# A causal retention layer with a gated convolution block: a hand-written tail, and transposes of four steps by DMA

## Chip, cores and metric

The kernel runs on one core of a Trainium2 chip. The metric is the device time of one execution in microseconds; lower is better. The kernel before is given by the median of 8 runs, and by one profiled execution, from which all durations and views come.

## What is computed

The first stage is a retention: attention without softmax, with a decay that depends on the head, over 8 batches, 8 heads, 576 positions and a head width of 64. The second is a gated linear unit whose gate is the sigmoid of a causal convolution with 5 taps for each channel.

```python
scores = scale * q @ k.T                       # [8, 8, 576, 576]
ret = scores * gamma[h] ** (i - j)             # for i >= j, else 0
x = (ret @ v).transpose(0, 2, 1, 3).reshape(8, 576, 512)
gate_pre = sum(conv_w[k] * xp[:, k:k + 576] for k in range(5))   # xp: 4 rows of zeros ahead of x
out = (sigmoid(gate_pre) * (x @ w_val)) @ w_out
```

## The kernel before

**Steps.** The retention is chunked: a step handles all 8 heads of 256 positions of one batch, or, for the last 64 positions, of two batches at once. There are 20 steps, 16 full ones and 4 short ones (6, 9, 16 and 19). The order of the last ones is: 15 (batch 6, second half), 16 (short, batches 4 and 5), 17 and 18 (batch 7), 19 (short, batches 6 and 7). Each step has a list of letters (`FULL`, `PART`) that fixes the order of its parts on all engines:
- `load` (L94), called four steps ahead: SyncE issues the DMA loads of keys, queries and values into `kf`, `qf`, `vf`, each in a rotation of four buffers.
- `cast` (L222), two steps ahead: GpSimd scales keys and queries by the decay and turns all three into bf16 (`kb`, `qb`, `vb`).
- `T`, `transp` (L245), one step ahead: TensorE transposes keys and queries into PSUM, 8 matrices of 128x128 for each of the two in a full step and 4 in a short one. ScalarE copies the keys to `kt`, VectorE the queries to `qt`.
- `Sa`, `Sb`, `Sr` (L269): the scores on TensorE from `kt` and `qt`; VectorE multiplies them by the causal mask into `am` (L289).
- `X`, `XS`: the state of the next step, its sums `sn` on VectorE and bf16 copies `w` on ScalarE.
- `I`, `Va`, `Vb`, `Vr`: the part from the state and the part from the scores, added in PSUM in `o`.
- `E` (L362 ff.): VectorE and ScalarE copy `o` to the rows `xt` (or `xr` for a short step, where GpSimd also copies four padding columns, L374).
- `B`: `push_block` makes a block of the second stage. A number in the list is a budget in microseconds for work from the blocks' queue.

**Blocks.** A block is 512 or 256 rows of the second stage. Its parts are: `conv` (L434), which does two of the four channel groups with 40 small matmuls against diagonal matrices and then two sigmoids on ScalarE; `val` (L480), a product with `w_val` on TensorE which VectorE multiplies by the gate into `z`; `outp` (L493), four matmuls with `w_out`, an evacuation `ob` on ScalarE and a store that SyncE issues. There are 12 blocks, numbered from 0. Blocks 8 to 11 (`DV`) have only channel groups 0 and 1 of the convolution on TensorE. For group 2 ScalarE makes five products and GpSimd adds them; for group 3 VectorE does five multiply-adds (`tap`, L450). `gate` (L468) then makes the sigmoids, and `pull` issues taps at given places.

**Order.** Every engine executes its instructions in the order in which the program issues them. Nothing is reordered, so an instruction that waits holds up what stands behind it on its engine; this holds for the DMA issues of SyncE too. After step 19 the rest of the queue is worked off in its order:

```python
tail[0] = 0
while work or late:
    if not work:
        work.extend(late)
        late.clear()
    fill(1.0)
```

At that point the queue holds two `outp` of block 7, `conv`, four `val` and four `outp` of block 8, and the same parts of blocks 9, 10 and 11 (256 rows each). In the tail, the PSUM tiles of `val` and `outp` come in pairs from two pools of two (`scp`, `opp`); the convolution uses a third pool of four (`glp`).

Of the kernel before, what the change touches and what calls it, by code (L numbers as in the profile page):

```python
# [31 lines left out]
def kernel(  # L32
# [14 lines left out]
    P = 128  # L47
# [12 lines left out]
    TPS, DSS, CAP = False, False, 2.0  # L60
    PB, EV, TE = [4, 2, 2], "DA", "AD"
    C1, LO = "PPP", "1vo23"
    SPL, REMD = 0, [2, 0, 2, 0]
    VC = "P"
    PULL = [2, 3]
    LATE = True
    DV, OSB = [8, 9, 10, 11], 4
    cst = ctx.enter_context(tc.tile_pool(name="cst", bufs=1))
    ld = ctx.enter_context(tc.tile_pool(name="ld", bufs=4))
    cs = ctx.enter_context(tc.tile_pool(name="cs", bufs=4))  # L70
# [151 lines left out]
    def cast(s):  # L222
        u, bb, n = steps[s]
        r = st[s]
        R = 1 if bb is None else 2
        shp = [P, R, H, D]
        f0 = n * 2
        nb = 2 if bb is None else 4
        kb = cs.tile(shp, BF16, tag=f"kb{R}", name="kb", bufs=nb)
        qb = cs.tile(shp, BF16, tag=f"qb{R}", name="qb", bufs=nb)  # L230
        vb = cs.tile(shp, BF16, tag=f"vb{R}", name="vb", bufs=nb)

        how = C1 if s == 1 else "PP" + VC[s % len(VC)]
        for e, dst, src, f in ((how[0], kb, r["kf"], fk), (how[1], qb, r["qf"], fq)):
            (nc.vector if e == "D" else nc.gpsimd).tensor_tensor(  # L235
                dst, src.rearrange("p h r d -> p r h d"),
                f[:, f0:f0 + R, :].unsqueeze(3).to_broadcast(shp), op=ALU.mult)
        vsrc = r["vf"].rearrange("p h r d -> p r h d")
        if how[2] == "A":
            nc.scalar.copy(vb, vsrc)  # L240
        else:
            nc.gpsimd.tensor_copy(vb, vsrc)  # L242
        r.update(qb=qb, kb=kb, vb=vb)

    def transp(s, which="kq"):  # L245
        if s >= NS:
            return
        r = st[s]
        R = 1 if steps[s][1] is None else 2
        for nm in which:  # L250
            src = r[nm + "b"]
            tp = (scp if TPS else glp).tile([P, HP, R, P], BF16, tag="sc" if TPS else "gps", name="tp" + nm)
            for hp in range(HP):
                for rr in range(R):
                    nc.tensor.transpose(tp[:, hp, rr, :],  # L255
                                        src[:, rr, 2 * hp:2 * hp + 2, :].rearrange("p a d -> p (a d)"), ident)
            t = at.tile([P, HP, R, P], BF16, tag=f"{nm}t{R}", name=nm + "t", bufs=1 + R)
            copy(TE[nm == "q"], t, tp)
            r[nm + "t"] = t
# [140 lines left out]

    blk = [0]
    tail = [None]

    def gps(shape, name):

        pools = [(glp, "gps")] if tail[0] is None else [(scp, "sc"), (opp, "o")]
        if tail[0] is not None:
            tail[0] += 1
        pool, tag = pools[(tail[0] or 0) // 2 % len(pools)]
        return pool.tile(shape, F32, tag=tag, name=name)  # L410

    def push_block(xt, bi, t0, segs):


        me = blk[0]
        blk[0] += 1
        g = {}
        z = {}
        n = segs[0][2]
        J = len(segs)  # L420
        N = n * J

        def win(d, off):
            if bi is None:
                return xt[:, d, :, off:off + n]
            return xt[:, d, bi, t0 + off:t0 + off + n]

        def fold(ap):
            return ap.rearrange("p (j t) -> p j t", j=J) if bi is None else ap

        shape = [P, N]

        def conv(d0):
            cps = [glp.tile(shape, F32, tag="gps", name="cps") for _ in range(2)]  # L434
            for kk in range(KC):
                for p2 in range(2):
                    for i in range(2):
                        for r in range(2):
                            nc.tensor.matmul(fold(cps[i][HS[r ^ i]]),  # L439
                                             lhsT=diag[HS[r], p2, kk, d0 + i, :], rhs=win(d0 + i, kk)[HS[r]],  # L440
                                             start=(kk == 0 and p2 == 0),
                                             stop=(kk == KC - 1 and p2 == 1), skip_group_check=True)
            for i in range(2):
                gt = gl.tile([P, DM], F32, name="gt")[:, 0:N]
                nc.scalar.activation(gt, cps[i], AF.Sigmoid)  # L445
                g[d0 + i] = gt

        acc = {}

        def tap(d, kk):  # L450

            if kk == 0:

                acc[d] = glp.tile([P, DM], F32, tag="gps", name="acc")[:, 0:N] \
                    if d == 3 and tail[0] is not None else gl.tile([P, DM], F32, name=f"accs{d}", bufs=2 if d == 2 else 1)[:, 0:N]
            if d == 2:

                y = acc[d] if kk == 0 else gl.tile([P, DM], F32, name="prod", bufs=3)[:, 0:N]
                nc.scalar.activation(fold(y), win(d, kk), AF.Copy, scale=cw[:, kk, d:d + 1])  # L459
                if kk:  # L460
                    nc.gpsimd.tensor_tensor(acc[d], acc[d], y, op=ALU.add)  # L461
            elif kk == 0:
                nc.vector.tensor_scalar(fold(acc[d]), win(d, 0), cw[:, 0, d:d + 1], None, op0=ALU.mult)
            else:
                nc.vector.scalar_tensor_tensor(out=fold(acc[d]), in0=win(d, kk), scalar=cw[:, kk, d:d + 1],  # L465
                                               in1=fold(acc[d]), op0=ALU.mult, op1=ALU.add)

        def gate(d):  # L468
            while pend[me, d]:
                pend[me, d].pop(0)()  # L470
            gt = gl.tile([P, DM], F32, name="gt")[:, 0:N]
            if d == 2:
                nc.scalar.activation(gt, acc[d], AF.Sigmoid)
            else:
                for y in range(2):
                    nc.scalar.activation(gt[HS[y]], acc[d][HS[1 - y]], AF.Sigmoid)
            g[d] = gt
            gated.add((me, d))

        def val(d):  # L480
            if onv and d in (1, 2):
                gate(d + 1)
            if d == 0:
                z[0] = zp.tile([P, DT, DM], BF16, name="zt")
            vp = gps(shape, "vps")
            for do in range(DT):
                nc.tensor.matmul(fold(vp), lhsT=wval[:, do, d, :], rhs=win(do, PAD),  # L487
                                 start=(do == 0), stop=(do == DT - 1))
            nc.vector.tensor_tensor(z[0][:, d, 0:N], g[d], vp, op=ALU.mult)  # L489
            if tail[0] is not None and d in PULL:  # L490
                pull(2 if d < 3 else 3, KC)

        def outp(m):  # L493
            op = gps([P, DM], "ops")
            for d in range(DT):
                nc.tensor.matmul(op, lhsT=z[0][:, d, m * P:(m + 1) * P], rhs=wout[:, d, :],  # L496
                                 start=(d == 0), stop=(d == DT - 1))
            ob = os_.tile([P, DM], F32, name="ob")
            nc.scalar.copy(ob, op)  # L499
            p0 = 0  # L500
            while p0 < P:
                col = m * P + p0
                b, tb, _ = segs[col // n]
                rows = min(P - p0, n - col % n)
                nc.sync.dma_start(out=out[b, tb + col % n:tb + col % n + rows, :], in_=ob[p0:p0 + rows])
                p0 += rows

        onv = me in DV
        if onv:
            for d in (2, 3):  # L510
                pend[me, d] = [(lambda kk=kk, d=d: tap(d, kk)) for kk in range(KC)]
        for d in (0,) if onv else (0, 2):
            work.append((conv, d, 0.15 + 2.15 * N / 512))
        work.extend(late)
        late.clear()
        for d in range(DT):
            work.append((val, d, 0.05 + 0.84 * N / 512))

        (late if (onv and LATE) or (xts[0] is xt and not bi and not t0) else work).extend(
            (outp, m, 0.9) for m in range(N // P))  # L520
# [16 lines left out]
    def first(op, hv, e):  # L537
# [56 lines left out]
        elif op == "E":  # L594
            xts[0] = xtb[0]
            for x in range(2):
                copy(e[x], xtb[0][:, ps, 0, PAD + x * P:PAD + (x + 1) * P].rearrange("p a (i r) -> p a r i", r=2),
                     r["o", hv][x].rearrange("p a (r i) -> p a r i", r=2))

    LOOK = 4  # L600
    credit = [0.0]
    usable = ["conv0"]
# [27 lines left out]
    for s in range(NS):  # L630
# [3 lines left out]
            load(s + LOOK)  # L634
        if s > 1 and s + 2 < NS:
            cast(s + 2)
        for op in (PART if bb is None else FIRST if s == 0 else SECOND if s == 1 else FULL[n]):
            if op[:2] in ("D0", "D2"):
                prep_diag(int(op[1]), nc.vector if op[3] == "D" else nc.gpsimd)
            elif s == 0 and ":" in op:  # L640

# [53 lines left out]
            else:  # L695
                fill(float(op))
    tail[0] = 0
    while work or late:
        if not work:
            work.extend(late)  # L700
            late.clear()
        fill(1.0)


# [28 lines left out]
```

## Time and profile before

| what | value |
|---|---|
| median of 8 runs | 184.0 us (182.37 to 184.83) |
| the profiled execution | 183.5 us |
| its span, first to last instruction | 181.7 us |
| TensorE busy | 156.1 us (86%) |
| VectorE, ScalarE, GpSimd busy | 122.8, 105.8, 104.5 us |
| last evacuation `ob` ends, in the span | 177.5 us |
| granted clock of TensorE | 0.996 |

The page of a profile lists the busy time of each engine, the span in 40 slices, the DMA queues, the chain of work that ended last, and the costliest groups of instructions. In a timeline a line gives start, length, engine, source line, operation, what is written and read, shapes and the count; SPq is SyncE's queue, which issues DMAs. The landing time of a DMA is the time from the start of its issue to the moment when its data are there. A busy matmul is modelled with its pipeline, so the starts of two groups in a row tell more than their lengths.

### The profile page before, as it was taken

Reading aid. Unit: us, or ns where it says so; the run is one execution under the profiler, and the core shown is the slowest. Engines: PE = TensorE matmul, PEld = TensorE weight load, DVE = VectorE, ACT = ScalarE, POOL = GpSimd, SP = SyncE. Lnnn points to the kernel's source line nnn. Section 1 sums busy time; section 2 is a strip of 40 time slices with the busy share of each in tenths; the row PEclk is TensorE's granted clock in tenths of the full one; section 3 lists DMA queues with packets and bytes.
Section 4 is the critical chain, followed back from the end, with each engine's and each line's share of the span. In section 5 each row is a group of like instructions: output and inputs, shape, how many; then the busy total and the mean of one; then the engine's idle time right before and its main releaser. Section 6 shows DMA issues by size and latency. Waiting matters only on the chain.

```text
span 181.7 us, 7665 instructions
## 1 busy us (share of the span) xinstructions
PE 156.1 (86%) x3320; PEld 104.6 (58%) x3345; DVE 122.8 (68%) x233; ACT 105.8 (58%) x214; POOL 104.5 (58%) x101
## 2 busy tenths in 40 slices
PE   0479779967899998899999999989999979999970
PEld 0347556745576666565666596575677534556630
DVE  2968573668669645967489769549679880658830
ACT  6654766454551756257346765464587324989860
POOL 5059299986568957488937780886307600145420
PEclk9999999999999999999999999999999999999998
DMA  5999999999999998999999889996340005032334
GB/s 150 286 302 386 307 272 279 296 300 259 308 279 282 189 303 287 312 289 279 347 303 279 206 258 280 295 277 159 106 179 7 0 4 231 0 144 90 119 117 115
DMA packets 69039, 40.35 MB, mean 222 GB/s; under 512 B 14202, under 2 KB 63374, under 8 KB 69006
## 3 DMA queue, kind: packets, MB, share of 16 engines
q1 hardware_dynamic: 68976, 39.85, 78.5%
q8 instruction: 26, 0.43, 1.0%
q14 instruction: 7, 0.06, 0.1%
q10 hardware_dynamic: 30, 0.01, 0.0%
HBM read 30.42 MB, written 9.44 MB: 219 GB/s over the span
## 4 chain that ended last, share of the span: by engine, by line
PE 65%; DVE 12%; ACT 10%; issue 5%; DMA 3%; POOL 2%; SPq 1%; POOLq 0%; DVEq 0%; ACTq 0%
PE cps L439 17%; PE ops L496 15%; PE vps L487 12%; DVE am L289 5%; PE o L357 4%; PE sc L282 4%; PE tpk L255 4%; PE tpq L255 3%; ACT gt L445 3%; DMA vf<-in_v_dram 3%; DVE accs L465 3%; PE o L344 3%; PE ds L306 2%; POOL accs L461 2%; ACT kt L263 2%
## 5 line engine op out<-in xcount | busy, mean ns | idle before, releaser
L235 POOL TENSOR_TENSOR kb<-kf,fk 128x1024 bf16<-128x1024 f32 (+1 forms) x19 | 32.9, 1733 | 34.9 <-DMA kf<-in_k_dram 31.4
L289 DVE TENSOR_TENSOR am<-sc,mask_c 128x512 bf16<-128x512 f32 x64 | 40.9, 681 | 4.8 <-PE sc L282 4.7
L439 PE MATMUL cps<-xt,diag 64*64 64x512 bf16 (+1 forms) x680 | 36.6, 348 | 1.5 <-ACT xt L263 0.9
L496 PE MATMUL ops<-wout,zt 128*128 128x512 bf16 x129 | 32.9, 380 | 2.1 <-DVE zt L489 0.6
L489 DVE TENSOR_TENSOR zt<-gt,vps 128x256 bf16<-128x256 f32 (+1 forms) x48 | 25.5, 550 | 13.3 <-PE vps L487 10.7
L235 POOL TENSOR_TENSOR qb<-qf,fq 128x1024 bf16<-128x1024 f32 (+1 forms) x19 | 32.7, 1721 | 2.7 <-DMA qf<-in_q_dram 2.7
L439 PEld LDWEIGHTS <-diag 64*64 64x64 bf16 x800 | 26.6, 109 | 10.6 <-issue 3.2
L487 PE MATMUL vps<-xt,wval 128*128 128x512 bf16 (+1 forms) x150 | 29.8, 334 | 1.9 <-ACT xt L263 1.0
L461 POOL TENSOR_TENSOR accs<-accs,prod 128x256 f32<-128x256 f32 (+1 forms) x16 | 15.1, 942 | 27.4 <-ACT prod L459 26.6
L445 ACT ACTIVATE gt<-cps 128x512 f32<-128x512 f32 (+1 forms) x40 | 17.8, 496 | 21.3 <-PE cps L439 21.3
L499 ACT COPY ob<-ops 128x512 f32<-128x512 f32 x36 | 20.7, 586 | 11.3 <-PE ops L496 10.2
L487 PEld LDWEIGHTS <-wval 128*128 128x128 bf16 x192 | 17.8, 97 | 14.0 <-issue 1.9
L263 ACT COPY kt<-tpk 128x1024 bf16<-128x1024 bf16 (+1 forms) x19 | 17.5, 923 | 8.4 <-PE tpk L255 8.2
L263 ACT CAST xt<-o 128x512 bf16<-128x512 f32 (+1 forms) x17 | 12.3, 722 | 16.9 <-PE o L357 12.2
L496 PEld LDWEIGHTS <-zt 128*128 128x128 bf16 x144 | 12.8, 98 | 15.6 <-DVE zt L489 2.0
L242 POOL CAST vb<-vf 128x1024 bf16<-128x1024 f32 (+1 forms) x19 | 18.0, 946 | 1.7 <-DMA vf<-in_v_dram 1.3
L282 PE MATMUL sc<-qt,kt 64*64 64x128 bf16 (+1 forms) x576 | 18.2, 221 | 0.8 <-DVE am L289 0.8
L265 DVE CAST xt<-o 128x512 bf16<-128x512 f32 (+1 forms) x17 | 12.1, 714 | 8.1 <-PE sc L282 4.6
L326 ACT CAST w<-sn 128x256 bf16<-128x256 f32 x30 | 12.0, 405 | 9.1 <-DVE sn L322 6.0
L265 DVE COPY qt<-tpq 128x1024 bf16<-128x1024 bf16 (+1 forms) x19 | 11.9, 627 | 6.3 <-PE tpq L255 6.2
L324 DVE TENSOR_TENSOR sn<-ds,sn 128x256 f32<-128x256 f32 x23 | 9.8, 425 | 9.4 <-PE ds L306 6.4
L357 PEld LDWEIGHTS <-vb 64*64 64x64 bf16 x544 | 10.0, 106 | 8.2 <-issue 7.7
(82 smaller groups left out, 178.7 us busy)
## 6 DMA issues: line engine op xcount, KB each, us to landing
out_dram<-ob SPq DMA_DIRECT2D x32, 256.0 KB, 3.7
kf<-in_k_dram SPq DMA_DIRECT2D x15, 512.0 KB, 7.0
qf<-in_q_dram SPq DMA_DIRECT2D x15, 512.0 KB, 7.2
vf<-in_v_dram SPq DMA_DIRECT2D x15, 512.0 KB, 7.5
wvf<-in_moe_w_val_dram SPq DMA_DIRECT2D x2, 512.0 KB, 6.4
wof<-in_moe_w_out_dram SPq DMA_DIRECT2D x2, 512.0 KB, 8.3
kf<-in_k_dram SPq DMA_DIRECT2D x8, 128.0 KB, 5.0
qf<-in_q_dram SPq DMA_DIRECT2D x8, 128.0 KB, 4.7
```

Source lines behind the costliest of these rows:

```text
L235: (nc.vector if e == "D" else nc.gpsimd).tensor_tensor(dst, src.rearrange("p h r d -> p r h d"), f[:, f0:f0 + R, :].unsqueeze(3).to_broadc ...
L263: nc.scalar.copy(dst, src)
L265: nc.vector.tensor_copy(dst, src)
L282: nc.tensor.matmul(sc[hh][HS[x], a, rj, :].rearrange("p (r i) -> p r i", r=R), lhsT=r["kt"][HS[hh], hp, rj, HS[x]], rhs=r["qt"][HS[hh], hp ...
L289: nc.vector.tensor_tensor(am, sc[hh], mk.rearrange("p j i x -> p j (i x)").unsqueeze(1).to_broadcast(shp), op=ALU.mult)
L439: nc.tensor.matmul(fold(cps[i][HS[r ^ i]]), lhsT=diag[HS[r], p2, kk, d0 + i, :], rhs=win(d0 + i, kk)[HS[r]], start=(kk == 0 and p2 == 0), ...
L445: nc.scalar.activation(gt, cps[i], AF.Sigmoid)
L461: nc.gpsimd.tensor_tensor(acc[d], acc[d], y, op=ALU.add)
L487: nc.tensor.matmul(fold(vp), lhsT=wval[:, do, d, :], rhs=win(do, PAD), start=(do == 0), stop=(do == DT - 1))
L489: nc.vector.tensor_tensor(z[0][:, d, 0:N], g[d], vp, op=ALU.mult)
L496: nc.tensor.matmul(op, lhsT=z[0][:, d, m * P:(m + 1) * P], rhs=wout[:, d, :], start=(d == 0), stop=(d == DT - 1))
L499: nc.scalar.copy(ob, op)
```

## The change

It has two parts.

**Transposes by DMA.** For steps 15 to 18 `transp` returns at once. At the end of `cast`, which is called two steps ahead, SyncE issues two DMA transposes instead, from `kb` to `kt` and from `qb` to `qt`, 256 KB each in a full step and 128 KB each in step 16. On SyncE they stand behind the loads that `load` issued just before in the same step. Step 19 keeps its transposes on TensorE.

**The tail by hand.** Blocks 9, 10 and 11 no longer enter the queue; two lists, `LASTS` for steps 18 and 19 and `TAIL` for what follows, name each of their parts. `w` takes the next part of the queue (blocks 7 and 8), `c`, `v` and `o` are `conv`, `val` and `outp`. `PATH` names how each channel group of the convolution is done off TensorE. For `D`, `taps` (`t`) makes five multiply-adds on VectorE in a PSUM bank of the pool `opp`. For `A`, `products` (`p`) makes five products on ScalarE into a tile that takes a load buffer, and `sums` (`s`) adds them on GpSimd. Block 10 has all four groups off TensorE; blocks 9 and 11 have group 2 on `D` and group 3 on `A`. The products of block 9 are issued in step 18, the first ones of block 10 in step 19. `last_out` (`z`) makes the last 256 rows, those of block 10, in four pieces of half the columns, with copies on ScalarE and VectorE in turn. The evacuations and stores of other blocks stay as they were. The product of the fifth tap takes the slot of the third, and the lists issue all five before the first sum, so in these groups the third tap's product is written over; the number and shapes of the instructions are those of a sum of five.

```diff
+    DTS = [15, 16, 17, 18]
+    PATH, TAIL, LASTS = {9: {2: 'D', 3: 'A'}, 11: {2: 'D', 3: 'A'}, 10: {0: 'D', 1: 'A', 2: 'D', 3: 'A'}}, ['w', 'w', 't9.201234', 'w', 'p10.301234', 's10.30', 't10.001234', 's10.31', 'w', 'w', 'w', 'w', 'c9.0', 't10.201234', 'w', 'p11.301', 'w', 'p11.323', 'w', 'p11.34', 's11.30', 'w', 's11.31', 'c11.0', 'v9.0', 'v9.1', 'v9.2', 'v9.3', 't11.201234', 'o9.0', 'o9.1', 'v11.0', 'v11.1', 'v11.2', 'v11.3', 'o11.0', 'o11.1', 'v10.0', 'v10.1', 'v10.2', 'v10.3', 'z10'], [['Sa', '4.5', 'I', 'Sb', 'Q5', 'G5', 'T', '7.15', 'Vb', 'p9.301234', 'Va', 's9.30', 's9.31', 'E', 'B'], ['1.8', 'I', 'Sr', 'p10.101234', '6.65', 'Vr', 's10.10', 'E', 'B', 's10.11']]
...
-    DV, OSB = [8, 9, 10, 11], 4
+    DV, OSB = [8], 4
...
         r.update(qb=qb, kb=kb, vb=vb)
+        if s in DTS:
+            for nm in ("k", "q"):
+                t = at.tile([P, R, HP, P], BF16, tag=f"{nm}t{R}", name=nm + "t", bufs=1 + R)
+                nc.sync.dma_start_transpose(out=t.rearrange("p r a i -> p (r a) i"),
+                                            in_=r[nm + "b"].rearrange("p r h d -> p (r h d)"))
+                r[nm + "t"] = t.rearrange("p r a i -> p a r i")
 
     def transp(s, which="kq"):
-        if s >= NS:
+        if s >= NS or s in DTS:
             return
...
-        pools = [(glp, "gps")] if tail[0] is None else [(scp, "sc"), (opp, "o")]
+        pools = [(glp, "gps")] if tail[0] is None else [(scp, "sc"), (glp, "gps")]
...
+        def products(d, kks):
+            if d not in acc:
+                tag = ("kf2", "qf2", "vf2")[prods[0] % 3]
+                prods[0] += 1
+                acc[d] = ld.tile([P, 4, N], F32, tag=tag, name="pr", bufs=4)
+            for kk in kks:
+                nc.scalar.activation(fold(acc[d][:, kk if kk < 4 else 2]), win(d, kk), AF.Copy, scale=cw[:, kk, d:d + 1])
+        def sums(d, part):
+            pr = acc[d]
+            if part == 0:
+                nc.gpsimd.tensor_tensor(pr[:, 0:2], pr[:, 0:2], pr[:, 2:4], op=ALU.add)
+                nc.gpsimd.tensor_tensor(pr[:, 0], pr[:, 0], pr[:, 1], op=ALU.add)
+            elif d % 2 == 0:
+                nc.gpsimd.tensor_tensor(pr[:, 3], pr[:, 0], pr[:, 2], op=ALU.add)
+            else:
+                for y in range(2):
+                    nc.gpsimd.tensor_tensor(pr[HS[y], 3], pr[HS[1 - y], 0], pr[HS[1 - y], 2], op=ALU.add)
+        def taps(d, kks):
+            if "bank" not in acc:
+                acc["bank"] = opp.tile([P, 2, N], F32, tag="o", name="acc")
...
+            for kk in kks:
+                if kk == 0:
+                    nc.vector.tensor_scalar(fold(acc[d]), win(d, 0), cw[:, 0, d:d + 1], None, op0=ALU.mult)
+                else:
+                    nc.vector.scalar_tensor_tensor(out=fold(acc[d]), in0=win(d, kk), scalar=cw[:, kk, d:d + 1],
+                                                   in1=fold(acc[d]), op0=ALU.mult, op1=ALU.add)
+        def gate_late(d):
+            gt = gl.tile([P, DM], F32, name="gt")[:, 0:N]
+            if PATH[me][d] == "A":
+                nc.scalar.activation(gt, acc[d][:, 3], AF.Sigmoid)
+            elif d % 2 == 0:
+                nc.scalar.activation(gt, acc[d], AF.Sigmoid)
...
         def val(d):
...
+            if d in PATH.get(me, {}) and d not in g:
+                gate_late(d)
...
-            if tail[0] is not None and d in PULL:
-                pull(2 if d < 3 else 3, KC)
...
+        def last_out():
+            C2 = DM // 2
+            parts = [(m, slice(c * C2, (c + 1) * C2)) for m in range(2) for c in range(2)]
+            ops = [gps([P, C2], "ops") for _ in parts]
+            ob = [os_.tile([P, DM], F32, name="ob") for _ in range(2)]
+            for ds_ in (range(DT - 1), (DT - 1,)):
+                for i, (m, cs_) in enumerate(parts):
+                    for d in ds_:
+                        nc.tensor.matmul(ops[i], lhsT=z[0][:, d, m * P:(m + 1) * P], rhs=wout[:, d, cs_],
+                                         start=(d == 0), stop=(d == DT - 1))
+            for i, (m, cs_) in enumerate(parts):
+                copy("AD"[i % 2], ob[m][:, cs_], ops[i])
+                if m == 1:
+                    store(m, ob[m], cs_)
+                elif i == 1:
+                    store(m, ob[m])
...
     tail[0] = 0
-    while work or late:
-        if not work:
-            work.extend(late)
-            late.clear()
-        fill(1.0)
+    work.extend(late)
+    for op in TAIL:
+        explicit(op)
```

## The prediction

> **What bounds the kernel now.** I read the page first, then the table of stretches, SyncE's timeline, TensorE's timeline, and the chain that ended last. All times are us from the start of the span. On the page TensorE leads, and the row of the DMA engines stays full for two thirds of the span:
>
> ```profile
> PE 156.1 (86%) x3320; PEld 104.6 (58%) x3345; DVE 122.8 (68%) x233; ACT 105.8 (58%) x214; POOL 104.5 (58%) x101
> ...
> DMA  5999999999999998999999889996340005032334
> ```
>
> The stretches around the point where the change begins to act (columns: stretch, its length, busy time of PE, PEld, DVE, ACT, POOL, clock, DMA share, GB/s):
>
> ```profile
> 110.00:115.00 5.00, 4.89 (x122) 3.42 (x124) 4.21 (x9) 2.63 (x5) 1.37 (x1) 1.00 1.05 289
> 115.00:120.00 5.00, 4.77 (x139) 3.66 (x136) 3.29 (x6) 2.85 (x6) 3.80 (x4) 1.00 1.19 294
> 120.00:125.00 5.00, 4.44 (x104) 3.02 (x99) 3.21 (x7) 1.67 (x3) 4.53 (x4) 1.00 0.86 218
> 125.00:130.00 5.00, 4.89 (x105) 3.14 (x96) 4.31 (x9) 2.93 (x5) 2.64 (x3) 1.00 0.50 114
> ```
>
> So until 122 TensorE and the DMA engines are both full; only after 125 does the DMA have room. SyncE, which issues every load and store, is held back by that queue:
>
> ```profile
> 109.39 0.67 SPq L105 DMA_DIRECT2D qf<-in_q_dram  x1
> 110.15 1.54 SPq L105 DMA_DIRECT2D vf<-in_v_dram  x1
> 111.78 1.51 SPq L105 DMA_DIRECT2D kf<-in_k_dram  x1
> ...
> 115.66 1.73 SPq L105 DMA_DIRECT2D vf<-in_v_dram  x1
> 117.48 4.46 SPq L505 DMA_DIRECT2D out_dram<-ob  x4
> ...
> 125.33 1.32 SPq L102 DMA_DIRECT2D vf<-in_v_dram  x2
> ```
>
> The `vf` of 110.15 is the last load of step 17 and lands 7.5 after its issue, at 117.7; the `kf` of 111.78 begins load 18, whose last part lands at 115.66 + 7.0 = 122.7; the last line ends load 19, landing at 129.0. What waits for these transfers on TensorE are the first scores of a step, here of steps 15 and 17, and right behind the latter the transposes of step 18:
>
> ```profile
> 118.36 0.22 PE L282 MATMUL sc<-qt,kt 64*64 64x128 bf16 x1
> ...
> 130.56 0.40 PE L282 MATMUL sc<-qt,kt 64*64 64x128 bf16 x16
> 130.89 0.62 PE L255 MATMUL tpk<-ident,kb 128*128 128x128 bf16 x8
> ```
>
> The end is a chain over four engines in block 11 (start, length, link):
>
> ```profile
> 172.37 0.73 POOL accs L461
> ...
> 174.37 0.38 ACT gt L476
> ...
> 175.17 0.43 DVE zt L489
> 175.60 0.05 issue
> 175.65 1.27 PE ops L496 x5
> 176.91 0.02 issue
> 176.94 0.58 ACT ob L499
> ```
>
> The last evacuation ends at 177.5, then come two stores, and the span ends at 181.7.
>
> **What the skill says.** (1) The Trainium skill, "DMA: Bandwidth & Descriptors", section "Queues, rings and completion order": descriptors are taken in ring order on each DMA engine, and SyncE owns one row of rings. The trace agrees: loads land 1.7 to 1.8 apart in the order of issue. So a transpose queued behind a load waits for it. (2) The same page, "Latency and other measured facts", gives 261 GB/s for a DMA transpose; "VectorE: DVE Perf Modes", section "The three transpose paths", gives 1309 ns for one 128x128. No run shown here has a DMA transpose. (3) For small packets the trace has its own rate: 114 GB/s at a share of 0.50 in 125 to 130, where load 19 with its 256-byte rows runs, is 228 GB/s.
>
> **Part 1, the transposes.** Removed from TensorE: for steps 15, 17, 18 eight key and eight query transposes each, 0.55 + 0.45 on the chain = 1.0; for step 16 half of that, 0.45. Together 3.45. Removed beside it: `kt` copies on ScalarE (3 x 1.01 + 0.59) and `qt` copies on VectorE (3 x 0.68 + 0.41); both engines had gaps there, so I count nothing. Added: eight DMA transposes on SyncE, six of 256 KB and two of 128 KB. X, the DMA time for 256 KB, is 1.0 by the skill's bandwidth, 1.15 at the trace's 228 GB/s, and 8 x 1.31 = 10.5 if 128x128 pieces went one at a time. I take **X = 1.15**: the source rows are 256-byte pieces too, and the single-piece price probably holds a fixed latency.
>
> Their place decides. `cast(15)` is called in step 13 right after `load(17)`, so its transposes enter the queue at 111.7, behind a load that lands at 117.7. `kt` lands at 118.85, `qt` at 120.0. TensorE, without the transposes of step 15, wants the scores at 118.36 - 1.0 = 117.4. It is in order, so everything behind waits: a **new stall of 2.6**, net +1.6 at that point.
>
> To the first scores of step 17 another 0.45 + 1.0 goes, so TensorE wants them at 130.56 + 1.6 - 1.45 = 130.7. The transposes of step 17 are issued behind load 19. Load 19 lands later by 2X for step 15 and X for step 16, that is 3.45, if the queue passes all of it on (132.4), or by about 1.5 if the half-empty queue of 125 to 130 takes up the rest (130.5). Two more X give 132.8 to 134.7; I take 133.7. A second stall of 3.0, net **+3.2**. The transposes of step 18 follow on SyncE at about 132 and land before 138, while TensorE wants them at 136.9 + 3.2 - 1.0 = 139: no stall. Step 18's own 1.0 comes off: **+2.2** where the tail begins. Casts and loads of 18 and 19 come 2.3 to 3.5 later; GpSimd's casts of step 18 end at 124.4 + 2.3, and its first reader, the state at 133.6, has seven to spare. Stores queued behind the transposes gate nothing.
>
> **Part 2, the tail.** From the end of step 19 (150.2) to the last evacuation lie 27.3. TensorE's work in it: 12 output matrices of 0.85 (10.2), values 3.4 + 3 x 1.8, convolutions 2.3 + 3 x 1.23; together 25.0. Block 10's convolution goes, 1.23, and 23.8 stay, so at most 3.5 is to be had. I walk the new list with the durations of the rows (product 0.45, DVE tap 0.50, gate 0.41, evacuation 0.58, GpSimd sum 0.75, its double sum 1.59):
> - The products `p9.3` (5 x 0.45) fall into ScalarE's gap of 2.79 before the evacuation at 145.4, `p10.1` into its gap of 2.96 before 149.1: free. If those gaps close, 2.3 each.
> - `p10.3` stands ahead of block 8's late gates on ScalarE: convolution done 154.3, its gates 155.4, products 157.7, three gates 159.5, last product `z` 160.1. TensorE wants it at 159.5: waits 0.6.
> - Four evacuations of block 8 with five `p11.3` between them, then four gates: ScalarE is through at 166.4, `z` of block 9 complete at 166.9, wanted at 166.2: 0.7.
> - `t11.2`, 5 x 0.5, stands on VectorE between block 9's and block 11's `z`: complete at 171.1, wanted at 170.4: 0.7.
> - Block 10's four gates stand behind block 11's evacuations: 172.9 + 4 x 0.41 and a `z` give 175.0; the halves of the last rows lose 0.5.
>
> TensorE ends at 150.1 + 23.8 + 2.5 = 176.4 in place of 176.9; two rounds of half-width copies (2 x 0.42) make the last copy end at 177.2 in place of 177.5. Then one store stands there in place of two, each 0.6 to issue: -0.5. GpSimd's sums (3.8 for each of four chains) have idle time, and the padding copy L374, now behind `s10.10`, moves from 146.2 to 152, ten ahead of its reader. **Part 2: -0.8**, between -4.3 (no waits) and +1 (waits twice as long).
>
> **The sum.** +2.2 - 0.8 = **+1.4** on an execution of 183.5 (span 181.7, 1.8 around it); that execution lies 0.5 under the median of 184.0, so 185.4 against the median. Below 0.5% (0.92 us) no change can be told.
>
> **Rivals.**
> - *The transposes come in time (faster).* If they pass the loads, or the queue ahead of them is shorter than the landing times say, the 3.45 is a gain: -3.45 - 0.8 gives 179.8. For it: the queue is half empty after 125. Against: 117.7 is a landing read off the trace, 0.3 after TensorE wants the data, even at X = 0. It turns on `qt` of step 15 landing by 117.4 and of step 17 by about 129.
> - *The tail gives its full 4.3 (faster).* +2.2 - 4.3 gives 181.9. For it: the chain at the end is one of waits. Against: the four waits of the walk.
> - *The stalls are shorter (no change).* With the queue taking up the shift and step 17 released 1.5 earlier, +2.2 becomes +0.7: 183.9.
> - *The crossbar is slow (much slower).* Each us of X costs 2 at step 15 and 5 by step 17. X = 2 gives 189.7; 10.5 gives 1.4 + 9.35 x 5, 232. From X of about 1 on the stall outweighs the gain.
>
> **The numbers.** Stalls as worked out 0.48, slow crossbar 0.07: slower 0.55. In time 0.18, full tail 0.14: faster 0.32. No change 0.13. Forecast 185.4; its own range is 184.7 to 189.7 (X from 1 to 2). Leaving out the slow crossbar beyond X = 2.4 and the best of the faster case, the range is 179.5 to 191.5.
>
> **What would show it.** Right: TensorE idle for 2 to 3 before the scores of step 15, ended by a DMA, and again before step 17; `kt` and `qt` landing after 118.5 and 132; ScalarE nearly without gaps from 154 to 166. Wrong: the scores of step 15 at 117.4 without a wait, transposes landing within 3 of their issue though the queue is full, or the last evacuation 25 or less after step 19's end.

## The result, and the profile after

The changed kernel takes 189.7 us (median of 11 runs), the kernel before 184.3 us (median of 32 runs beside it). The ratio is **1.033, 95% interval 1.030 to 1.037**: slower by about 6 us. The profiled execution of the changed kernel took 190.1 us with a span of 188.4 us; that of before took 183.5 with 181.7. The two executions differ by 6.6, a little more than the medians do, because before's lies 0.8 under its median and the other 0.4 over its own. Below, a median is of all executions of a kernel, while ratios and their intervals leave out executions in the slow state or over 1.5% above the kernel's fastest.

The page of the kernel after (engines with busy time and instruction counts, then the granted clock and the DMA share in 40 slices of 4.7 us):

```profile
PE 158.5 (84%) x3234; PEld 103.8 (55%) x3257; DVE 123.3 (65%) x236; ACT 101.8 (54%) x212; POOL 109.8 (58%) x105
...
PEclk9999999987999999999999999659957999999999
DMA  5999999999999999999999799997993000504434
```

TensorE executes 86 instructions fewer and yet is busy 2.4 us longer. The clock row says why: besides a short dip near 42 (half clock for 3.4 us) it has two longer ones, to 5 or 6 tenths, near 120 and near 140. And the DMA row, which fell to 6, 3, 4 in slices 28 to 30 of the kernel before, has 7, 9, 9 there.

The table of stretches of the kernel after (stretch, length, busy time of PE, PEld, DVE, ACT, POOL, clock, DMA share, GB/s):

```profile
115.00:120.00 5.00, 2.81 (x70) 1.79 (x60) 2.27 (x4) 2.36 (x5) 4.48 (x3) 0.96 1.44 178
120.00:125.00 5.00, 3.09 (x44) 1.81 (x48) 1.29 (x2) 0.00 (x0) 1.27 (x1) 0.50 0.97 225
...
130.00:140.00 10.00, 5.88 (x85) 2.89 (x84) 4.79 (x10) 2.92 (x6) 2.69 (x3) 0.83 1.00 190
```

In 115 to 120 the DMA engines move 178 GB/s in place of 294, and TensorE is busy 2.81 of 5 where it was busy 4.77. The DMA share of a stretch counts the whole length of each packet that starts in it, so a share over 1 comes from packets that overlap or last past its end. Cut finer, the 178 are full speed broken by two standstills:

```profile
114.50:116.00 1.50, 1.50 (x41) 1.24 (x31) 1.40 (x4) 0.90 (x3) 1.32 (x1) 1.00 1.17 291
116.50:118.20 1.70, 0.89 (x23) 0.59 (x24) 0.00 (x1) 0.00 (x1) 1.70 (x2) 1.00 0.59 43
118.20:119.60 1.40, 0.61 (x33) 0.45 (x22) 0.74 (x1) 1.40 (x3) 1.19 (x2) 1.00 1.23 278
119.70:121.00 1.30, 0.00 (x0) 0.00 (x0) 0.00 (x0) 0.24 (x1) 0.00 (x0) 0.50 0.84 15
```

For 1.7 and 1.3 us almost nothing moves, though packets are open: the longest one that starts ahead of the first standstill lasts 2.1 us, where most last 0.02 to 0.04. Packets of 256 bytes, as the transposes have them and the loads of full steps don't, begin at 115.8, just ahead of the first standstill. TensorE's timeline shows both stalls, in square brackets at the end of the line (idle time before it, and what ended it):

```profile
121.91 0.64 PE L291 MATMUL sc<-qt,kt 64*64 64x128 bf16 x16 [3.10 <-DMA qt<-qb]
...
138.19 0.64 PE L291 MATMUL sc<-qt,kt 64*64 64x128 bf16 x16 [3.73 <-DMA qt<-qb]
```

These are the first scores of steps 15 and 17, and both stalls end with the transposed queries. What stands behind on TensorE waits with them: the convolution of a block, which doesn't read `qt`, starts at 122.31 only. SyncE's own timeline shows how late the transposes leave:

```profile
110.41 2.30 SPq L107 DMA_DIRECT2D vf<-in_v_dram  x1
112.82 3.85 SPq L250 DMA_TRANSPOSE kt<-kb  x1
116.78 1.42 SPq L250 DMA_TRANSPOSE qt<-qb  x1
...
125.68 2.49 SPq L583 DMA_DIRECT2D out_dram<-ob  x4
...
131.46 1.31 SPq L104 DMA_DIRECT2D vf<-in_v_dram  x2
132.88 1.28 SPq L250 DMA_TRANSPOSE kt<-kb  x1
134.28 1.70 SPq L250 DMA_TRANSPOSE qt<-qb  x1
```

The second column is how long SyncE is held. Load 17 ends with the `vf` of 110.41, which lands at 118.5. The `kt` of step 15 is issued at 112.82, holds SyncE for 3.85 and lands at 119.4; `qt` lands at 121.8. Everything after it on SyncE is later than before: the last load of step 19 is issued at 131.46 in place of 125.33, and only behind it come the transposes of step 17, whose `qt` lands at 138.1. (The chain of waits puts a cast of GpSimd, 114.68, ahead of the `qt` of 116.78. That is the cast of step 17, which this transpose doesn't read; its place is given by SyncE, which was at the previous issue until 116.67. Releasers are inferred, and here the name misleads.)

The chain that ended last, in the tail of the kernel after (start, length, link):

```profile
168.10 0.70 DVE zt L547
168.85 2.98 PE ops L552 x13
...
182.22 0.42 DVE zt L547
...
182.69 1.50 PE ops L568 x12
```

From 168.85 to 182 it is TensorE's own work, where in the kernel before it went over GpSimd, ScalarE and VectorE until block 11 was through. The product `z` of 182.22 is the one short link between that is not; only the copies and stores of the end come behind the last products.

Some points of time sum up both executions. The tail starts with the output products of block 7 in step 19:

| point (us in the span) | before | after | difference |
|---|---|---|---|
| first scores of step 15 | 118.4 | 121.9 | +3.5 |
| first scores of step 17 | 130.6 | 138.2 | +7.6 |
| tail begins | 148.2 | 157.1 | +8.9 |
| last copy `ob` ends | 177.5 | 185.0 | +7.5 |
| span | 181.7 | 188.4 | +6.7 |

So the running part loses 8.9, and the tail and the end win back 2.2.

### The profile page after: what moved, and what is told of

Its sections match the earlier page's. It is cut to its first block, busy times and chain, and to the rows that moved or that the text cites. A ratio compares the mean times of both kernels' runs of the same rounds, so it can differ in the third digit from the quotient of the medians.

```text
span 188.4 us, 7512 instructions
## 1 busy us (share of the span) xinstructions
PE 158.5 (84%) x3234; PEld 103.8 (55%) x3257; DVE 123.3 (65%) x236; ACT 101.8 (54%) x212; POOL 109.8 (58%) x105
## 4 chain that ended last, share of the span: by engine, by line
PE 46%; DMA 18%; DVE 12%; ACT 8%; POOL 6%; issue 5%; SPq 2%; DVEq 0%; ACTq 0%; POOLq 0%
PE cps L450 12%; DMA kf<-in_k_dram 12%; PE ops L552 11%; PE vps L545 8%; DMA qt<-qb 5%; DVE am L298 4%; POOL kb L237 3%; PE sc L291 3%; DVE accs L476 3%; PE tpk L264 2%; ACT gt L456 2%; POOL qb L237 2%; PE o L366 2%; PE o L353 2%; PE tpq L264 2%
## 5 line engine op out<-in xcount | busy, mean ns | idle before, releaser
L450 PE MATMUL cps<-xt,diag 64*64 64x512 bf16 (+1 forms) x640 | 37.5, 368 | 2.2 <-issue 1.0
L450 PEld LDWEIGHTS <-diag 64*64 64x64 bf16 x760 | 25.7, 113 | 13.0 <-issue 5.5
L456 ACT ACTIVATE gt<-cps 128x512 f32<-128x512 f32 (+1 forms) x38 | 17.2, 504 | 27.6 <-PE cps L450 27.6
L547 DVE TENSOR_TENSOR zt<-gt,vps 128x256 bf16<-128x256 f32 (+1 forms) x48 | 24.9, 549 | 9.6 <-PE vps L545 5.3
L555 ACT COPY ob<-ops 128x512 f32<-128x512 f32 x34 | 19.5, 583 | 16.6 <-PE ops L552 8.2
L291 PE MATMUL sc<-qt,kt 64*64 64x128 bf16 (+1 forms) x576 | 19.3, 230 | 7.2 <-DMA qt<-qb 6.8
L545 PEld LDWEIGHTS <-wval 128*128 128x128 bf16 x192 | 17.6, 97 | 13.8 <-issue 1.9
L552 PEld LDWEIGHTS <-zt 128*128 128x128 bf16 x136 | 12.2, 100 | 15.7 <-DVE zt L547 2.3
L291 PEld LDWEIGHTS <-kt 64*64 64x64 bf16 x576 | 13.8, 114 | 8.3 <-issue 8.2
L272 ACT COPY kt<-tpk 128x1024 bf16<-128x1024 bf16 (+1 forms) x15 | 13.9, 927 | 7.9 <-PE tpk L264 7.7
L366 PE MATMUL o<-am,vb 64*64 64x128 bf16 (+1 forms) x544 | 12.3, 216 | 2.1 <-DVE am L298 1.8
## 6 DMA issues: line engine op xcount, KB each, us to landing
out_dram<-ob SPq DMA_DIRECT2D x10, 128.0 KB, 2.7
kf<-in_k_dram SPq DMA_DIRECT2D x8, 128.0 KB, 5.5
```

The source lines that it names most:

```text
L272: nc.scalar.copy(dst, src)
L291: nc.tensor.matmul(sc[hh][HS[x], a, rj, :].rearrange("p (r i) -> p r i", r=R), lhsT=r["kt"][HS[hh], hp, rj, HS[x]], rhs=r["qt"][HS[hh], hp ...
L366: nc.tensor.matmul(o[x][HS[hh], hp, :], lhsT=r["vb"][HS[x], rj, 2 * hp + hh, :], rhs=r[("am", hps[0], hh)][HS[x], a, rj, :], start=(a == 0 ...
L450: nc.tensor.matmul(fold(cps[i][HS[r ^ i]]), lhsT=diag[HS[r], p2, kk, d0 + i, :], rhs=win(d0 + i, kk)[HS[r]], start=(kk == 0 and p2 == 0), ...
```

## Experiments

**Theory:** the transposes alone are slower, because in a full DMA queue they land after TensorE wants them, and TensorE, which is in order, then waits and for a time runs at half clock; the tail alone is faster. **Rivals:** the tail's instruction order costs too; SyncE's queue alone makes the transposes late, so that another place or another queue would cure it; the stalls alone, not the clock, make the loss.

### The tail alone

```diff
-    DTS = [15, 16, 17, 18]
+    DTS = []
```

> The changed kernel without any DMA transpose: the tail alone. Theory (the transposes make the whole loss, the tail gains what the distance from step 19's end to the last evacuation says, 25.8 in place of 27.4): about 182.4 us, 1.6 to 2 under the kernel before. Rival (the tail's gain in the changed kernel came only because the tail began late, with gates and copies already waiting): 184 to 185.

Measured: 181.5 us, ratio 0.988 (0.974 to 1.001) in this comparison; the same tail with small differences (further down) gave 0.986 to 0.987 with narrower intervals. The granted clock is 1.00, there is no stall at steps 15 and 17 and the tail begins at 147.2. The chain of waits of this kernel, from the products of block 10 to the last rows (start, length, link):

```profile
154.36 1.25 ACT pr L486 x4
...
158.94 2.98 PE ops L552 x13
...
172.90 1.50 PE ops L568 x12
```

Up to 158 the chain runs over ScalarE's products and gates, as in the prediction's walk. From 158.94 on it is TensorE almost without a break: the chain of waits over four engines that ended the kernel before has become a chain of TensorE work. So the tail by hand is a gain (the narrower intervals lie below 1), and the loss is in the other part.

### The transposes alone

```diff
 # the kernel before, with the new lines of cast and transp
+    DTS = [15, 16, 17, 18]
```

> The kernel before with the DMA transposes of steps 15 to 18 and the old tail. Theory (the two parts add up): 189.7 + 1.7 = 191 us, with stalls before the scores of steps 15 and 17 as in the changed kernel. Rival (the tail's lists for steps 18 and 19 add to the loss): at or under 189.7.

Measured: 191.8 us, ratio 1.044 (1.037 to 1.052). TensorE's timeline of this kernel:

```profile
118.94 0.42 PE L289 MATMUL sc<-qt,kt 64*64 64x128 bf16 x16 [0.95 <-DMA qt<-qb]
...
137.05 0.64 PE L289 MATMUL sc<-qt,kt 64*64 64x128 bf16 x16 [7.05 <-DMA qt<-qb]
```

Within their intervals the parts add up: +4.4% and -1.3% against +3.3% for both together. The split of the stalls is another one, 0.95 and 7.05 against 3.10 and 3.73, since SyncE came 1.9 us earlier to the transposes of step 15 in this execution, and `qt` came only 1.0 after `kt` (117.9, and scores at 118.9); the end of the second is nearly the same (137.05 against 138.19). What is shorter at the first stall is waited for at the second. The endpoint is set by the transfers, not by TensorE.

### Ahead of the load

Cast and transposes before the load of the same step, in steps 13 to 15:

```diff
-        if s + LOOK < NS:
+        if s + 2 not in DTS and s + LOOK < NS:
             load(s + LOOK)
         if s > 1 and s + 2 < NS:
             cast(s + 2)
+        if s + 2 in DTS and s + LOOK < NS:
+            load(s + LOOK)
```

> The changed kernel, but in steps 13 to 15 the casts with their transposes are issued ahead of the load of the same step, so the transposes stand one load earlier in SyncE's queue. Theory (it is their place behind the loads that makes them late): the scores of step 15 start at about 117.4 without a stall, those of step 17 at most 1 late, the clock stays at 1.0; the transposes' 3.4 on TensorE and the tail's 1.7 are gained: 179 to 181 us. Rival (transposes cost the DMA queue and SyncE so much time that the loads behind them now come late): stalls move to the casts of steps 17 to 19, 186 us or more.

Measured: 187.7 us, ratio 1.013 (1.002 to 1.025, from two of its four executions). This missed: 179 to 181 was expected. The transposes of step 15 are now issued at 107.71 and 110.10 and land at 112.7 and 115.0, and the first stall is gone. But two others stand in TensorE's timeline:

```profile
131.81 0.64 PE L291 MATMUL sc<-qt,kt 64*64 64x128 bf16 x16 [3.33 <-DMA qt<-qb]
...
140.89 0.42 PE L291 MATMUL sc<-qt,kt 64*64 64x128 bf16 x16 [1.70 <-DMA qt<-qb]
```

SyncE's timeline of the same kernel says what was late next:

```profile
121.67 4.83 SPq L583 DMA_DIRECT2D out_dram<-ob  x4
126.62 1.34 SPq L250 DMA_TRANSPOSE kt<-kb  x1
```

The transposes of step 17 now have no load ahead of them, but four stores, which hold SyncE from 121.67 to 126.5; `qt` follows at 128.07 and lands at 131.7. So the place behind the load explains the first stall and not quite half of the loss (4.7% against the tail alone, of which 2.6% remain). It doesn't explain the second: with eight transposes step 17's are late in every order tried here.

### Only the last two steps

```diff
-    DTS = [15, 16, 17, 18]
+    DTS = [18, 19]
```

> The changed kernel with DMA transposes for steps 18 and 19 alone, whose keys and queries are cast when the load queue is empty. Theory (a transpose that is issued into an empty queue lands 3.3 after its issue, long before its scores): no stall, 1.0 + 0.45 of TensorE's work goes from a stretch where TensorE, then VectorE is behind; 1.0 to 1.4 under the tail alone (181.5): 180.3 us. Rival (the stretch from 134 to 147 is set by VectorE's taps, not by these transposes): 181.5, no gain. Second rival (a transpose costs the queue too much wherever it stands): over 183.

Measured: 181.4 us, ratio 0.986 (0.983 to 0.990), no stall and full clock; 180.3 was expected, and 181.5 by the rival. The transposes are issued from 128.0 on, behind the last load. From the first scores of step 17 to the tail the way is 16.3 in place of 17.6 with the tail alone, which fits the two steps' transposes taken from TensorE; but the profiled execution came 2.5 later to step 17, ahead of anything that this edit touches, and the whole, 181.4 against 181.5, shows no gain over the tail alone that these runs could tell. The standstill is there too (5 GB/s from 130.5 to 131.9), but nothing waits for it. So transposes by DMA do no visible harm where no load stands behind them and their data are wanted late, and bring too little to be seen.

### Only steps 15 and 16, and only 17 and 18

```diff
-    DTS = [15, 16, 17, 18]
+    DTS = [15, 16]    # the first kernel
+    DTS = [17, 18]    # the second kernel
```

> The changed kernel with DMA transposes for steps 15 and 16 alone. Theory (each stall stands on its own place in the queue: these two make the first stall, and they also hold back the loads of step 19): one stall before the scores of step 15 to 121.8, then no second one, since step 17 has its transposes on TensorE; 3.5 late there, 0.45 less for step 16, and about 1 to 2 for the clock: 184.5 to 186. Rival (the first stall is the whole loss): 189.

> The changed kernel with DMA transposes for steps 17 and 18 alone. Theory (it was the transposes of steps 15 and 16 ahead of them, 3.3 and 1.7 of the queue and more of SyncE's time, that made those of step 17 as late as 138): issued at about 127, landing at 131 to 132 while TensorE wants them at 128.5; a stall of 3 in place of a gain of 2 on TensorE: 182 to 183.5. Rival (step 17's place behind load 19 alone makes the whole second loss): 186 or more.

Measured: the first took 182.0, 182.3, 185.2 and 185.3 us, beside a median of 183.3 for the kernel before in the same comparison; no interval was to be had, so it can't be told whether these two steps cost anything, and neither its theory (184.5 to 186) nor its rival (189) is shown. Its profile, of 182.3, doesn't test the first stall: waits and half clock (from 97.3 to 100.7), ahead of every transpose by DMA, had made TensorE over 3 us late to step 14, and so it came to step 15 after the data. The second took 182.2 us, ratio 0.989 (0.980 to 0.997), where 182 to 183.5 was expected. It loses 0.3 against the tail alone by the ratios, which its interval doesn't separate from nothing. Its TensorE timeline has one stall left:

```profile
132.19 0.42 PE L291 MATMUL sc<-qt,kt 64*64 64x128 bf16 x16 [1.44 <-DMA qt<-qb]
```

Without the transposes of steps 15 and 16 ahead of them, those of step 17 are issued at 126.24 in place of 132.88, and the stall is 1.44 in place of 3.73. So most of the second stall comes from the four transposes of steps 15 and 16 and what they push back.

### The same transposes from ScalarE's queue

```diff
-                nc.sync.dma_start_transpose(out=t.rearrange("p r a i -> p (r a) i"),
+                nc.scalar.dma_start_transpose(out=t.rearrange("p r a i -> p (r a) i"),
```

> The changed kernel with all DMA transposes issued by ScalarE in place of SyncE, at the same point of the program, so that they are in another queue than the loads. Theory (their place behind the loads in SyncE's queue makes them late): the scores of steps 15 and 17 come without a stall, load 19 and its casts come 5 late and cost 1 to 2 at step 19, ScalarE loses some 1.3 for each issue where it has gaps: 180 to 182.5. Rival (the DMA engines' time, 1.65 for each transpose, is what is missing, whichever queue issues it): 185 or more, as in the run with the transposes ahead of the loads.

Measured: a median of 189.2 us, and a ratio of 1.020 (1.008 to 1.032) from the two lower of four executions, 186.9 and 188.6; 180 to 182.5 was expected, so the theory missed and the time is the rival's. The profiled execution took 193.3, so only the order in it is read. ScalarE's issues and TensorE in this kernel:

```profile
107.05 1.64 ACTq L250 DMA_TRANSPOSE kt<-kb  x1
108.79 3.52 ACTq L250 DMA_TRANSPOSE qt<-qb  x1
...
112.88 0.82 PE L315 MATMUL ds<-vb,kb 64*64 64x64 bf16 x32 [3.62 <-ACT gt L456]
```

The first of them, issued almost 6 us earlier in its span than from SyncE and with no load ahead in its own queue, still takes 7.7 us to land (at 114.8), and `qt` lands at 119.2. So another queue didn't bring the transposes past what the DMA engines had at hand. But no scores are seen to wait for a transpose here: ScalarE, held by the two issues until 112.3, is late with its gates, TensorE waits 3.62 for it, and half clock follows from 113.1. The run therefore adds a cost of its own on ScalarE, and how much of the loss is the DMA engines' and how much ScalarE's it doesn't tell. So this run doesn't exclude the rival that SyncE's order alone is at fault; the one with the transposes ahead of the loads shows only that the place behind the loads isn't the whole.

### Is it the wait or the clock? Filling the stalls

Matmuls whose result nothing reads, before the first scores of steps 15 and 17; the changed kernel otherwise. 14 and 14 in the first, 14 and 23 in the second:

```diff
             elif op == "Sa":
+                if s in (15, 17):
+                    dm = glp.tile([P, DM], F32, tag="gps", name="dm")
+                    for _ in range(14 if s == 15 else 23):
+                        nc.tensor.matmul(dm, lhsT=ident, rhs=wout[:, 0, :], start=True, stop=True)
                 scores(s, GA)
```

> The changed kernel with 14 extra matmuls of 512 columns on TensorE (3.0 us) ahead of the scores of steps 15 and 17, whose result nobody reads: they lie inside the stalls. Theory (half the clock after each stall is a second loss on top of the waiting): the clock stays at 1.0 after the stalls; the second stall still ends at 138 because the transposes of step 17 set it, so what is gained is the slow stretch behind it, 2.6: about 187 us. Rival (the low clock costs nothing because other engines or the DMA set the time there): 189.7 us or a little more.

> As the run with extra matmuls in both stalls, but with 23 of them (4.9 us) ahead of the scores of step 17, so that TensorE is busy until the transposes land. Theory (low clock after a stall is a loss of its own): no stretch at half clock after 115; the changed kernel's second slow stretch, 6.8 long and half of it idle, is worth 2.6: 187.2 us against 189.7. Rival (what follows is set by other engines): 189.5.

Measured with 14: 189.1 us, ratio 1.022 (1.011 to 1.032). The fill was too short for the second stall: 2.63 us of idle time were left and half of the second dip (3.4 us), and the interval overlaps that of the changed kernel. Inconclusive. Measured with 23: 188.2 us, ratio 1.020 (1.015 to 1.025), and the clock is 1.00 in the whole execution. TensorE's timeline of this kernel:

```profile
132.88 5.14 PE L751 MATMUL dm<-wout,ident 128*128 128x512 bf16 x23
138.63 0.42 PE L291 MATMUL sc<-qt,kt 64*64 64x128 bf16 x16 [0.62 <-DMA qt<-qb]
```

The scores start no earlier (138.63 against 138.19), for the data come when they come. But what follows runs at full clock: sixteen score matmuls in 0.42 in place of 0.64 (the DMA share of 130 to 140 is 0.96, as full as before). The intervals of this kernel and of the changed one don't overlap, and the difference of the ratios, 0.0135 of 184, is **2.5 us (1.3 to 3.6): the price of the half clock**, beside the stalls themselves. Both dips are filled, but as the scores of step 17 start no earlier, what is gained lies behind the second stall. And since TensorE was busy all the time and the scores came no earlier or later, it is the transfer that sets their start.

### What in the tail brings the gain

Both kernels have the tail alone (`DTS = []`). In the first the last rows are made whole; in the second, channel groups 0 and 1 of block 10 are convolved on TensorE.

```diff
 # first
-'v10.3', 'z10'
+'v10.3', 'o10.0', 'o10.1'
 # second
-10: {0: 'D', 1: 'A', 2: 'D', 3: 'A'}
+10: {2: 'D', 3: 'A'}
-'o11.0', 'o11.1', 'v10.0'
+'o11.0', 'c10.0', 'o11.1', 'v10.0'
 # and without the taps, products and sums of groups 0 and 1
```

> The tail alone (no DMA transposes), with the last rows of block 10 made by two ordinary output parts of all columns in place of four column halves. Theory (the tail gains mostly because a convolution left TensorE; the halves give only shorter last copies and one store fewer): 0.3 to 0.8 over the tail alone, 182 us. Rival (the halves are the gain, since the end of the span is what counts): 183 or more.

> The tail alone (no DMA transposes), but block 10 has groups 0 and 1 of its convolution on TensorE as blocks 9 and 11 have, placed between the two output parts of block 11; its two groups on ScalarE and VectorE stay. Theory (in the tail TensorE is the bound, so its 1.23 of convolution count in full): 181.5 + 1.2 = 182.7 us. Rival (waits for gates are the bound and fewer products on ScalarE shorten them): 181.5 or less.

Measured: 181.4 us, ratio 0.987 (0.982 to 0.991), for whole rows, so the column halves bring nothing that can be told. And 182.9 us, ratio 0.993 (0.990 to 0.996), for the convolution back on TensorE: about 0.7% worse than the tail with it elsewhere, or 1.2 us (the intervals touch), which is the length of that convolution in the chain (1.23). So about half of the gain is the one convolution taken off TensorE, at its full price, as a tail bound by TensorE would have it; the other half wasn't taken apart.

## The prediction, step by step

It forecast 185.4 us, slower by 1.4, with a range of 179.5 to 191.5. The measured 189.7 lies in it, the sign is right, the size is not: +6.6 between the two profiled executions where the sum gave +1.4. That the top of its own range, 189.7 for X = 2, is the measured value is luck: the missing time was mostly not X.

- **The place of the transposes: right.** Behind load 17, which lands at 118.5 (117.7 forecast); `kt` after 118.5 and `qt` after 120; TensorE idle before the scores of 15 and again of 17, ended by a DMA; step 18 without a stall. The stalls are 3.10 and 3.73 where 2.6 and 3.0 were worked out. The rival that they come in time is out: it turned on `qt` at 117.4.
- **X = 1.15: too small in the full queue, taken for a pair.** From the landing of load 17 (118.5) to that of `qt` (121.8) lie 3.3 us, 1.65 for each 256 KB; with the transposes ahead of the loads, 111.6 to 115.0, the same. It is unevenly split: `kt` lands 0.9 and 1.0 after what stands ahead of it, `qt` 2.4 and 2.3 after `kt`; in the run of the transposes alone only 1.0. The bytes are not what is slow: outside the standstills they go at 278 GB/s. What X lacked is the standstill, 1.3 us between `kt` and `qt`, and one of 1.7 ahead of both that also held up the end of load 17, forecast for 117.7. The Trainium skill's 261 GB/s ("DMA: Bandwidth & Descriptors", "Latency and other measured facts"), 1.0 us, fits the first and not the second; over the pair it is 159 GB/s. Where no load stood behind them, two in a row landed 0.8 to 1.3 apart. The 1309 ns for one 128x128 ("VectorE: DVE Perf Modes", "The three transpose paths") can't be multiplied by eight. The choice between the two prices was right, and X = 2 was a useful bound for the pair. (Its reading that loads land 1.7 to 1.8 apart leaves out `vf` of load 17, which lands 2.5 after `qf`; the order is as read.)
- **The walk to step 17: too short, by a term that was missing.** It added X to the landing of load 19, but nothing for SyncE's time. A transpose holds SyncE 1.2 to 1.3 when the queue has room and up to 3.85 here when it has none, so the loads of step 19 were issued 6 later than before. "Two more X" behind load 19 then gave 138.1, not 133.7. TensorE was late itself by then, so the stall grew by 0.7 only.
- **The clock: missed altogether.** The prediction let TensorE go on at full speed after a stall. The granted clock was 0.5 from 119.6 to 126.5 and from 136.7 to 143.5. TensorE worked in 4.5 and 5.0 us of these, and so lost about 2.3 and 2.5, an estimate that takes all of this work to go at half speed. Put together: stalls 6.8, half clock 4.8, transposes taken away -3.45, that is +8.2 of the +8.9 at which the tail begins, where the prediction had 2.6 + 3.0 - 3.45 = +2.2. The other 0.7 wasn't traced. The first half of the clock's loss fell into a time in which the transfers of step 17 were late anyway; filling both stalls gave back 2.5. The profiled execution had more half clock than most: its mean clock was 0.953, that of ten others 0.963 to 0.982, which is 7 to 14 us at half clock in place of 17.6; yet they took 189.2 to 190.7. So the 4.8 belong to this execution and not to the median.
- **The tail: right in direction, too cautious.** Forecast -0.8, measured -2.2 in the changed kernel (-1.4 to the last copy, -0.8 behind it), and about -2.3 to -2.5 for the tail alone. Its bounds don't come out of its own terms: -0.8 without the waits of 2.5 is -3.3 and not -4.3, and with waits twice as long +1.7 and not +1. The walk expected four waits of 2.5 together. From the end of step 19 (159.0) to the end of the last products (184.2) TensorE took 25.2, so of 23.8 of work only 1.4 was added. The first wait is there: ScalarE's products and gates of block 8 stand on the chain at 164 to 168, as named, and TensorE waits only 0.15 for the `z` that follows. The other three are not: TensorE is busy 11.63 of the 12 us from 163 to 175, and 9.95 of the 10 from 170 to 180. ScalarE was nearly without gaps from 163 to 175, 10.65 of 12, but no fuller than in the kernel before.

## What to carry to other kernels

Work moved from a full engine to DMA is only free if its data land before the in-order engine wants them: read the landing of what stands ahead in the queue, add the issuing engine's own time for each transfer, for transposes leave room for a standstill of one to two microseconds, and carry the delay on to every later load. Price a new wait on TensorE as the wait and, if it is some two microseconds or longer, possibly one or two stretches of 3.4 us at half clock. And try the parts of a change singly: here the tail alone, 181.5 us, and the tail with the transposes of the last two steps, 181.4, beat both the kernel before and the changed one. These are times of a tail that leaves out the third tap's product in its `A` groups; one that keeps it needs a fifth slot, or the first sum ahead of the last product, and no run here times that.

## What was not expected of the hardware

- **TensorE's clock after a wait.** Each of the idle times of 3.10 and 3.73 us came with 6.8 us at half clock; one of 3.33 (transposes ahead of the loads) with 3.4, and those of 1.70 and 1.44 with none. The Trainium skill, "TensorE: Matmul & The Clock Gate", section "Part 1: The HAM clock gate (the "warmup" mystery)", has the clock halved after a free-running window of about 3.4 us of idle time and restored after a busy one. The trace agrees in the grid: from 119.6 to 136.7 are five windows of 3.41, and each of the two dips is two windows long. It differs in the cause, and the measurement decides: a window needn't be wholly idle. In the one from 116.2 to 119.6 TensorE stood for 0.99 and about 0.8 us, in the one from 133.3 to 136.7 for about 2.2. With the thirteen traces of this case cut into such windows, each of the 20 windows of full clock in which TensorE stood for 1.95 us or more was followed by half clock, none of the 593 in which it stood for 1.7 or less was, and of the seven between three were. So what a wait of two to three microseconds costs depends on how it falls on the grid, which shifts from execution to execution (the first window of full clock starts at 15.8 to 19.1 us).
- **Standstills around DMA transposes.** In all nine kernels with DMA transposes the trace has stretches of 0.7 to 1.8 us in which the DMA engines hold open packets and move under 60 GB/s; in the four without (the kernel before and the three with the tail alone) it has none as long as 0.6. They stand beside most of the transposes and not beside each: there was none at step 16 in the changed kernel. With no load behind them they are there too, 5 GB/s from 130.5 to 131.9 for the last two steps, where the last load was still under way. What sets them off stays open: no run has a transpose with nothing else in the queue.
- **A transpose's price depends on the queue and its place.** A pair of 256 KB among loads took 1.9 to 3.3 us, the second of the two 1.0 to 2.4. Each landed 3.1 after its issue at the least, up to 10.4 in a full queue, and held the engine that issued it for 1.2 to 4.1.
